# Decay sums and an evacuation moved to VectorE, the second weight loaded later, and a new fixed order, in a kernel of recurrent attention, Fourier mixing and an MLP

## Chip, cores and metric

One core of a Trainium2 chip. The metric is the device time of one execution in microseconds (us). Runs come with a state: a run over 1.5% above the fastest of the same kernel in its call is called slow and is left out of ratios. A **ratio** is the mean time of one kernel's fast runs over the mean of the other's fast runs of the same rounds, so it is not quite the ratio of the medians quoted beside it, which are of all runs, slow ones too. Intervals are of 95%.

Engines: PE is TensorE (matmuls; PEld its weight loads), DVE is VectorE, ACT is ScalarE, POOL is GpSimd, SP is SyncE, which issues loads and stores. PEclk is the share of full speed that the chip's throttle granted to TensorE.

## The reference

Four batches, eight heads, 768 steps, head size 48. A recurrence with a decay per step, then a 2D FFT over steps and features, a layer norm and an MLP (384 to 1536 to 384).

```python
for t in range(S):
    cur = einsum('bhd,bhe->bhde', u * k[t], v[t])
    y[t] = einsum('bhd,bhde->bhe', r[t], state + cur)
    state = w[t][..., None] * state + einsum('bhd,bhe->bhde', k[t], v[t])
x = y with the heads side by side                    # 4 x 768 x 384
u = x + real(fft(fft(x, axis=1), axis=2))
un = (u - mean) / sqrt(var + 1e-6)
out = u + relu(un @ w_ch1) @ w_ch2
```

## The kernel before

The recurrence is done in 24 chunks of 128 steps (6 to a batch; chunk 7 is the second of batch 1). Every operation of the program, 1540 of them, is recorded with its engine and dependencies; a constant list ORDER then says in which sequence they stand, and a constant BANKS which of the 8 PSUM banks each of 347 tiles gets. Each engine runs its own operations strictly in that sequence, and waits at each for what it depends on. So a wait on one engine holds up all that stands behind it.

The parts that the change touches, with cuts (`...`):

```python
def load(b, c):                                   # the SP queue
    for n in "wkrv":
        o = op("sp", "load", f, r=["W1"] if b*NC + c == NC + 1 and n == "w" else (), ...)

ws, WN = [], ((6, "w"), (6, "w"))                 # both weights are asked for when w of chunk 6 landed
def weights():                                    # GpSimd's queue
    ws.append(op("pool", "loadw", ... W1 ...)); ws.append(op("pool", "loadw", ... W2 ...))

KHD, DIAG, RKD, PRE, EVD = range(6), range(5), (), range(0), range(0)
TCD, SAD = range(12, 24), range(12, 24)

def attention(b, c):                              # n: the chunk's number
    tcd = n in TCD
    op("act", "ln", L = Ln(w))
    tce = g.tile(pool); tci = tce if tcd else g.tile(pool)
    op("pe", "cum", matmul(tce, MSK, L))          # L614: sums of decays up to a step
    if not tcd:
        op("pe", "cum", matmul(tci, NLE, L))      # L619: the other sum, by a second matmul
        op("act", "exp", exp of tce in place)
    ...
    if tcd:                                       # the other sum from the first, on DVE
        op("dve", "tcd", e2 = tce + L)            # L636
        op("act", "exp4", ...); op("act", "exp", ...); op("act", "expn", e2 = exp(-e2))
    elif early: ...
    else:
        op("act", "exp2", e2 = exp(tci))          # L648
    ...
    op("dve", "rh", rh = tce * r)                 # L663
    ...

def mix(b, ...):                                  # FFT, layer norm, MLP
    for kb in range(NC): ...
        op("dve", "uf", uf = mixed + x)
        op("pe", "trn", transpose of un) ...      # or, for the blocks of TUN, by a DMA on SP (L882)
        elif n in EVD: op("dve", "evd", unt <- PSUM)
        else:          op("act", "ev384", unt <- PSUM)
    for hf in range(2):
        for j in range(NJ):
            op("pe", "m1", 3 matmuls of W1 and unt)      # L920; L926 in the changed kernel
            ... relu to ht
        for x in range(3):
            for jq in range(3):
                op("pe", "m2", 4 matmuls of ht and W2)   # L941; L947 in the changed kernel
            op("dve", "osb", ...); op("sp", "store", ...)

NW2 = 5                                           # warm-up matmuls ahead of the first real work
...
g.arrange(ORDER, BANKS)
```

## Time and profile before

| | before |
|---|---|
| time, median of 3 runs | 196.43 us (195.55 to 197.74) |
| span of the profiled run | 193.5 us |
| busy: PE, DVE, ACT, POOL | 93%, 79%, 71%, 61% |
| mean granted clock | 1.00 |

In the page's span line and engine lines, x is the number of instructions. In a row of the windows, a stretch of time is followed by its length and the busy us of each engine in it. The lines on which the prediction rests are shown in it. One more is needed later, the shares of the chain of work that ended last:

```profile
PE 43%; DVE 34%; SPq 8%; DMA 6%; ACT 5%; issue 2%; DVEq 0%
```

### The profile page before, as it was taken

How to read it: one execution, taken by the hardware profiler on the slowest of the kernel's cores; microseconds unless marked ns; L12 is line 12 of the kernel's file. 1: busy time of each engine (PE TensorE's matmuls, PEld its weight loads, DVE VectorE, ACT ScalarE, POOL GpSimd, SP SyncE). 2: the span in 40 equal slices, each digit the busy share in tenths (PEclk: the TensorE clock that was granted, in tenths of full speed). 3: DMA queues.
4: the chain of work that ended last, by engine and by line, in shares of the span. 5: the costliest groups of instructions: out<-in, count | busy, mean ns of one | idle time of the engine just before them, and what ended most of it. 6: DMA issues, size and time to landing. Idle time of an engine off the chain costs nothing.

```text
span 193.5 us, 4590 instructions
## 1 busy us (share of the span) xinstructions
PE 180.0 (93%) x1730; PEld 114.7 (59%) x1730; DVE 152.1 (79%) x356; ACT 137.8 (71%) x333; POOL 118.3 (61%) x148
## 2 busy tenths in 40 slices
PE   4979899999999999998999998999979999979994
PEld 2446466755666566565767675666656566545663
DVE  8799689697258999999999999999989969800043
ACT  7899867656997794499999897488855344769400
POOL 1679789920689996899799988639375461000000
PEclk9999999999999999999999999999999999999999
DMA  5999899699989989889899991242735020140024
GB/s 118 225 217 188 170 218 172 116 179 201 208 176 237 207 176 244 160 193 233 186 211 227 199 226 32 54 125 54 160 68 122 3 81 2 38 149 0 0 81 163
DMA packets 113351, 28.14 MB, mean 145 GB/s; under 512 B 108209, under 2 KB 112946, under 8 KB 113330
## 3 DMA queue, kind: packets, MB, share of 16 engines
q1 hardware_dynamic: 111378, 25.50, 62.3%
q0 software_dynamic: 1952, 2.36, 7.4%
q8 instruction: 13, 0.21, 0.4%
q14 instruction: 8, 0.07, 0.1%
HBM read 23.59 MB, written 4.72 MB: 146 GB/s over the span
## 4 chain that ended last, share of the span: by engine, by line
PE 43%; DVE 34%; SPq 8%; DMA 6%; ACT 5%; issue 2%; DVEq 0%
PE bank L920 15%; PE bank L941 12%; SPq L440 7%; DVE ah L708 6%; DVE xf L404 5%; DVE x L862 4%; DVE osb L946 4%; DVE bst L866 3%; DMA unt<-un 3%; DMA in_w<-in_w_dram 3%; PE bank L821 3%; DVE x L773 2%; ACT ht L929 2%; DVE rh L663 2%; DVE xa L404 2%
## 5 line engine op out<-in xcount | busy, mean ns | idle before, releaser
L920 PE MATMUL bank<-unt,w 128*128 128x384 bf16 x288 | 52.5, 326 | 2.4 <-DMA unt<-un 2.4
L941 PE MATMUL bank<-w,ht 128*128 128x384 bf16 (+1 forms) x300 | 54.0, 320 | 0.2 <-DVE ah L708 0.2
L929 ACT ACTIVATE ht<-bank 128x384 bf16<-128x384 f32 x92 | 40.9, 505 | 9.8 <-PE bank L920 9.7
L920 PEld LDWEIGHTS bank<-unt,w 128*128 128x128 bf16 x288 | 26.4, 97 | 18.8 <-issue 3.2
L941 PEld LDWEIGHTS bank<-w,ht 128*128 128x128 bf16 x300 | 27.5, 98 | 15.3 <-DVE ah L708 0.4
L404 POOL TENSOR_TENSOR rk<-in_r,in_k 128x384 f32<-128x384 f32 x24 | 24.1, 1004 | 16.8 <-DMA in_r<-in_r_dram 15.8
L708 DVE TENSOR_TENSOR ah<-bank,msk 128x512 bf16<-128x512 f32 x48 | 31.2, 682 | 2.3 <-PE bank L703 2.2
L946 DVE SCALAR_TENSOR_TENSOR osb<-bank,rstd,x 128x384 f32<-128x384 f32 (+1 forms) x25 | 14.6, 595 | 21.7 <-PE bank L941 21.6
L404 POOL TENSOR_TENSOR rk<-rk,ub 128x384 f32<-128x384 f32 x24 | 24.2, 1013 | 0.6
L404 POOL TENSOR_TENSOR kh<-in_k,e 128x384 bf16<-128x384 f32 x18 | 18.3, 1019 | 5.8 <-ACT e L640 3.6
L404 POOL TENSOR_TENSOR vtd<-in_v,dc 128x384 f32<-128x384 f32 x24 | 19.8, 829 | 2.8 <-DVE dc L655 2.7
L663 DVE TENSOR_TENSOR rh<-bank,in_r 128x384 bf16<-128x384 f32 x24 | 13.2, 552 | 5.3 <-ACT bank L621 5.0
L418 ACT ACTIVATE un<-x,agg 128x384 bf16<-128x384 f32 x18 | 10.8, 619 | 9.3 <-DVE agg L868 9.1
L988 PE MATMUL bank<-wz 128*128 128x384 bf16 x53 | 13.8, 379 | 2.5 <-DVE wz L415 2.5
L655 DVE TENSOR_REDUCE dc<-rk 128x8 f32<-128x384 f32 x24 | 13.0, 545 | 1.9 <-POOL rk L404 1.8
L418 ACT ACTIVATE vb<-in_v 128x384 bf16<-128x384 f32 x24 | 12.7, 531 | 1.7 <-DMA in_v<-in_v_dram 1.2
L418 ACT ACTIVATE lb<-in_w 128x384 bf16<-128x384 f32 x24 | 12.6, 534 | 1.6 <-DMA in_w<-in_w_dram 1.3
L866 DVE BATCH_NORM_STATS2 bst<-x 128x6 f32<-128x384 f32 x24 | 12.7, 553 | 0.1
L821 PE MATMUL bank<-cs,xf 128*128 128x193 bf16 (+2 forms) x54 | 11.1, 257 | 1.4 <-DVE xf L404 1.2
L693 ACT ACTIVATE rtb<-bank 128x512 bf16<-128x512 bf16 x19 | 11.3, 605 | 1.4 <-PE bank L680 1.2
L862 DVE TENSOR_TENSOR x<-bank,x 128x384 f32<-128x384 f32 x24 | 12.3, 542 | 0.0
L695 ACT ACTIVATE ktb<-bank 128x512 bf16<-128x512 bf16 x19 | 11.2, 602 | 0.7 <-PE bank L684 0.7
(129 smaller groups left out, 362.3 us busy)
## 6 DMA issues: line engine op xcount, KB each, us to landing
in_w<-in_w_dram SPq DMA_DIRECT2D x24, 192.0 KB, 3.8
in_k<-in_k_dram SPq DMA_DIRECT2D x24, 192.0 KB, 3.8
in_r<-in_r_dram SPq DMA_DIRECT2D x24, 192.0 KB, 3.8
in_v<-in_v_dram SPq DMA_DIRECT2D x24, 192.0 KB, 3.9
out_dram<-osb SPq DMA_DIRECT2D x23, 192.0 KB, 2.3
w<-in_moe_w_ch_dram POOLq DMA_DIRECT2D x2, 1152.0 KB, 10.4
out_dram<-osb SPq DMA_DIRECT2D x2, 96.0 KB, 1.7
unt<-un SPq DMA_TRANSPOSE x6, 3.0
```

Of the source, the lines that this page charges most:

```text
L404: return shared(lambda e: e.tensor_tensor(out=o, in0=a, in1=b, op=f))
L418: return lambda e: e.activation(o, a, f, **kw)
L663: op("dve", "rh", lambda e: e.tensor_tensor(out=rh[:, :, 0:D], in0=ps(tce)[:, 0:DM].rearrange("t (h d) -> t h d", d=D), in1=rt[:, :, :], o ...
L708: masked[n] = op("dve", "ah", lambda e, x=x: e.tensor_tensor(out=ah[:, x:H:2, :], in0=ps(ta[x])[:, :].rearrange("p (h t) -> p h t", t=128) ...
L821: return e.matmul(ps(t)[:, k0:k1], xf[:, f, off:off + 128], tab[:, s, k0:k1], start=a, stop=z, skip_group_check=True)
L862: op("dve", "uf", lambda e, kb=kb, t=t: e.tensor_tensor(out=uf[:, kb, 0:DM], in0=ps(t)[:, 0:DM], in1=uf[:, kb, 0:DM], op=ALU.add), r=[t], ...
L866: op("dve", "bns", lambda e, kb=kb, bs=bs: e.bn_stats(bs[:, :], uf[:, kb, 0:DM]), r=[("X", b % 3, kb)], w=[("BST", n % 4)])
L920: ins = e.matmul(ps(t)[:, 0:384], W1[:, m, 128 * j:128 * j + 128], unt[:, m, :], start=(m == 0), stop=(m == NM - 1))
L929: op("act", "ev384", lambda e, j=j, t=t, ht=ht: e.activation(ht[:, j, :], ps(t)[:, 0:384], ACTF.Relu), r=[t], w=[("HT", q % 2, j)])
L941: ins = e.matmul(ps(t)[:, c0:c1], ht[:, j, 128 * x:128 * x + 128], W2[:, j, c0:c1], start=(j == 0), stop=(j == NJ - 1))
L946: op("dve", "osbh" if n_end else "osb", lambda e, kb=kb, t=t, o=o, c0=c0, c1=c1: e.scalar_tensor_tensor(out=o[:, c0:c1], in0=ps(t)[:, c0:c ...
L988: ins = e.matmul(ps(tw)[:, 0:384], WZ[:, 0:128], WZ[:, :])
```

## The change

The intent: from 44 to 60 us VectorE and GpSimd are half idle, because the load of the second weight holds up the inputs of chunk 7; later VectorE is full and TensorE waits for it. So ask for that weight later, and fill the hole with VectorE work that relieves TensorE, ScalarE and PSUM. The diff, cut to its core:

```diff
-            o = op("sp", "load", f, r=["W1"] if b * NC + c == NC + 1 and n == "w" else (), ...
+            o = op("sp", "load", f, r=[WG[b * NC + c]] if b * NC + c in WG and n == "w" else (), ...
-    ws, WN = [], ((6, "w"), (6, "w"))
+    ws, WN, WG = [], ((6, "w"), (9, "w")), {7: "W1"}
-    KHD, DIAG, RKD, PRE, EVD = range(6), range(5), (), range(0), range(0)
+    KHD, DIAG, RKD, PRE, EVD, PRM = range(6), range(5), (), (), range(3), ()
-    TCD, SAD = range(12, 24), range(12, 24)
+    TCD, SAD = range(6, 24), range(12, 24)
-    NW2 = 5
+    NW2 = 6
 ORDER, BANKS: new from the first entry to the last (1546 operations, 341 PSUM tiles)
```

PRM and PRE are empty, so what else the diff adds for them does nothing.

## The prediction

> **What bounds the kernel now.** I read the page first, then the work by stretch, the chain of work that ended last, the waits of 36 to 60 us, and the issues of the load queue.
>
> ```profile
> span 193.5 us, 4590 instructions
> PE 180.0 (93%) x1730; PEld 114.7 (59%) x1730; DVE 152.1 (79%) x356; ACT 137.8 (71%) x333; POOL 118.3 (61%) x148
> DMA  5999899699989989889899991242735020140024
> ```
> No engine is idle enough to make one bound for the whole kernel, and the DMA engines are full for the first 24 slices (116 us). PE's 93% is too high: its matmuls overlap. The chain shows
>
> ```profile
> 89.43 5.47 PE bank L920 x33
> ```
> which is 166 ns for a 384-column matmul whose row on the page says 326. So I count PE by 166 ns and look for where it waits.
>
> ```profile
> core 0: us, PE busy (x) PEld busy (x) DVE busy (x) ACT busy (x) POOL busy (x), PEclk, DMA share, GB/s
> 40.00:44.00 4.00, 3.72 (x34) 2.09 (x33) 3.93 (x12) 2.91 (x6) 0.00 (x0) 1.00 1.27 184
> 44.00:48.00 4.00, 4.00 (x28) 2.45 (x28) 3.05 (x10) 2.56 (x6) 0.00 (x0) 1.00 1.27 204
> 48.00:52.00 4.00, 4.00 (x34) 2.57 (x33) 1.11 (x2) 4.00 (x12) 1.99 (x2) 1.00 1.03 205
> 52.00:56.00 4.00, 4.00 (x34) 2.46 (x33) 1.02 (x2) 4.00 (x13) 3.70 (x5) 1.00 1.05 208
> 56.00:60.00 4.00, 4.00 (x43) 2.61 (x42) 3.13 (x6) 3.33 (x10) 3.23 (x5) 1.00 0.90 178
> 70.00:80.00 10.00, 9.57 (x113) 6.52 (x110) 9.86 (x21) 5.06 (x14) 7.86 (x10) 1.00 0.93 201
> 80.00:90.00 10.00, 8.99 (x99) 5.70 (x98) 9.88 (x24) 9.09 (x20) 9.67 (x13) 1.00 0.95 206
> ```
> Here is the hole. From 44 to 60 us DVE does 8.31 us of work in 16: 7.7 us idle, and GpSimd does nothing from 40 to 48. From 60 on DVE is full (19.36, 19.84, 19.35 and 19.66 us in the four 20 us stretches from 60 to 140) and PE has short stalls. The chain agrees: it runs through DVE from 60.3 to 88, through PE's MLP matmuls (L920, L941) from 89 to 113, again through DVE from 113 to 131. So work that DVE puts off at 44 to 60 is paid for later. Why the hole is there, the waits of that window tell:
>
> ```profile
> POOL rk L404 <- DMA in_r<-in_r_dram: 9.2, 1, 9.2
> DVE rh L663 <- ACT bank L621: 3.9, 2, 2.8
> DVE dc L655 <- POOL rk L404: 1.8, 1, 1.8
> ```
> and the load queue, where the column after the start is the length of an issue:
>
> ```profile
> 37.84 1.76 SPq L440 DMA_DIRECT2D in_r<-in_r_dram  x1
> 39.65 3.55 SPq L440 DMA_DIRECT2D in_v<-in_v_dram  x1
> 43.24 4.14 SPq L440 DMA_DIRECT2D in_w<-in_w_dram  x1
> 47.42 1.18 SPq L440 DMA_DIRECT2D in_k<-in_k_dram  x1
> ```
> The second weight is issued at 36.5 and lands 11.6 us later, at 48.1. The loads of chunk 7 go out in the same time and are held up: issues take up to 4.14 us instead of the median of 0.71, and r of chunk 7, issued at 37.8, is used only at 48.9.
>
> **What the Trainium skill says.** "DMA: Bandwidth & Descriptors", section "Issuing engines are not separate DMA queues": DMAs started by sync or gpsimd run on the same 16 engines and interleave. The trace agrees: the GpSimd queue's weight stretches the sync queue's loads as shown. "Perfetto Trace Analysis", section "Identifying the Most-Contended Engine": matmul busy share is a poor measure, matmuls being pipelined; the trace agrees (326 against 166 ns). "VectorE: DVE Perf Modes", section "The TRN2 errata", gives 120 + FD cycles for a one-per-cycle operation out of PSUM; at 384 elements and 0.96 GHz that is 525 ns. The decay sum L636 shows 551 ns, but two in a row take 0.97 us in the chain, so 0.48 each of the engine's time. I use 0.47.
>
> **The change, part by part.**
>
> Decay sums of batch 1 (chunks 6 to 11) on DVE. Removed from PE: 6 matmuls L619, 6 x 0.166 = 1.0 us. On ACT, 6 exponentials L648 (5 x 0.534 + 0.491 = 3.2 us) give way to 6 of L642 (0.529) and 5 short ones L640 (0.18): 3.2 + 0.9 = 4.1 us, so +0.9. Added on DVE: 6 x 0.47 = 2.8 us. One PSUM bank less is held per chunk. Latency to kh grows by about 0.5 us per chunk; it is hidden if the order runs ahead.
>
> Evacuation of the first half of batch 0: 3 copies of 128x384 leave ACT (L901, 0.42 us apart) and come to DVE, 3 x 0.47 = 1.4 us. They stand just before the first L920 (43.9 us), where DVE is full (3.93 of 4.00). In the new order they come after the statistics, so I expect the first L920 about 0.5 us later, at 44.4.
>
> Second weight after load 9: it is asked for when w of chunk 9 has landed. Chunks 7 and 8 (4 loads of 0.71 to 1 us of issue each) and w of 9 then take 36.8 to about 47, and r of chunk 7 lands at its normal 3.8 us, at about 42 instead of 48.9. The weight lands at 47 + 11.6 = 59 or so. In the new order all 24 first-layer matmul groups of batch 0 come ahead of the first L941 (before: at 52.7), so at 59 nobody waits for it yet. The bytes are the same; only their order changes.
>
> One more warm-up matmul: 0.17 us, where PE has slack. The parts named PRE and PRM have empty lists and do nothing. The W1 wait of the loads is the same one, spelled otherwise.
>
> Sum by engine: PE -0.8, DVE +4.2, ACT about -0.3.
>
> Fixed order anew. I counted what stands between the first L920 and the first finished L941 block (osb) in the new order. PE: 24 groups of 3 L920 (72 x 0.166 = 12.0), chunks 7 to 9 and half of 10 (1.65 us each: about 5.7), 12 L941 (2.0): 19.7 us. DVE: 46 instructions: 5 decay sums, 19 more of 384 elements (4 rh, 4 dc, 4 x, 4 relu, 2 uf, 1 fold) and 2 statistics at 0.47, 6 masks (L708) at 0.60, 8 half state products (L739) at 0.36, 6 small ones, together about 20 us. ACT: about 19.6 us. So the hole is to be filled, and all three engines are planned full at once. Before, DVE had done 8.9 us of work by the same output, at 60.3.
>
> Putting times on it: if nothing stalls, that output comes at 44.4 + 19.7 = 64. At that place DVE has finished chunk 9; in the kernel before it got there at 73.7, having done 3.0 us of other work by then, so at 70.7 like for like. DVE would be 6.7 ahead, including the extra sums. PE would be ahead by little: the hole was DVE's and GpSimd's; PE was 4.00 of 4.00 there. But three engines planned full with in-order queues don't run at 100%; I put 2 to 3 us of stalls there, an estimate by choice from PE's stalls in the stretches 80 to 90 (1.0 us of 10). That leaves DVE 4 us ahead and PE about 1 behind. What PE then wins is its stalls behind DVE between 60 and 88 and between 113 and 131: 0.4 and 1.0 us in the two rows shown, more when counted by 166 ns; I put 4 to 5 us. Some 3 of them go: -1 + 3 = 2, plus 0.3 from the removed matmuls and something from the second DVE-bound stretch. I expect 2.5 us less, at the end of which the tail (last transposes by DMA, then 72 matmuls of L920 and L941) is as before.
>
> **The rivals.**
> First, DVE becomes the bound by more: 4.2 us more work on an engine full from 60 to 140. If the hole isn't filled (ACT, 4.00 of 4.00 from 48 to 56, feeds rh; L663 waited 3.9 us for it there), the end moves by up to +3 us: 199. Against it: the new order puts chunk 7's exponentials ahead of the first-layer evacuations on ACT.
> Second, the full gain: stalls are few and PE keeps DVE's lead, 5 us or more less: 191. For it: the chain is DVE for 46 of the 71 us from 60 to 131. Against: PE's MLP stretch, 89 to 113, can't shrink.
> Third, the late weight is waited for: L941 stalls on W2 if load 9 lands after 50. Each us late past 62 is a us of PE: +1 to +3. Against: the first-layer matmuls and three chunks stand ahead of it.
> Fourth, the gain is swallowed by the tail: the DMA transposes (3.95 us in the chain before 173) and the fixed PE order: 196, no change.
>
> **Range and chances.** Before 196.43. The expected 2.5 us less (with the scatter of 1% of three runs) gives 193.8. The third and fourth rivals make 196 to 197, the second 191; so 190.8 to 196.8. Faster by over 2% needs 192.5: 0.27. Slower by over 2% needs the first rival in full: 0.05. Within 2%: 0.68.
>
> **What would show it.** Right: r of chunk 7 used at 42 to 43; GpSimd busy from there; DVE at least 13 of 16 us in 44 to 60; W2 landed by 60 with no wait of L941 for it; 6 L619 left; DVE full until about 128 instead of 131; chain in 60 to 88 partly PE. Wrong: DVE still idle by 5 us in 44 to 60 (stalls behind ACT), L941 waiting for the weight, or DVE's lead at 70 lost by 130.

## The result, and the profile after

| | before | after |
|---|---|---|
| time, median of 4 runs each | 197.09 us (195.55 to 199.55) | 189.83 us (188.88 to 191.57) |
| ratio of fast runs | | 0.9667 [0.9556, 0.9778] |

The result is correct and faster by 3.3%, outside the predicted range. In a later call the same kernel gave 0.9735 [0.9654, 0.9816], with 2 of 6 runs fast.

From the page of the changed kernel:

```profile
span 187.7 us, 4599 instructions
PE 179.4 (96%) x1725; PEld 115.5 (62%) x1725; DVE 155.4 (83%) x365; ACT 136.8 (73%) x335; POOL 118.6 (63%) x148
PEclk9969999999999999999999999999999999999999
PE 71%; SPq 8%; DVE 7%; DMA 7%; ACT 4%; issue 1%; DVEq 0%
```

DVE has 3.3 us more to do (155.4 against 152.1; 4.2 were forecast), PE 0.6 less, and the span is 5.8 us shorter. The chain went from one third DVE to nearly all PE. And there is a 6 in the clock's row, where before all slices had a 9: the third slice, 9.4 to 14.1 us. Both points get an experiment.

Work by stretch in the changed kernel, for the stretches shown of the kernel before:

```profile
core 0: us, PE busy (x) PEld busy (x) DVE busy (x) ACT busy (x) POOL busy (x), PEclk, DMA share, GB/s
40.00:44.00 4.00, 3.78 (x39) 2.36 (x38) 4.00 (x13) 2.98 (x7) 1.00 (x1) 1.00 1.11 222
44.00:48.00 4.00, 4.00 (x27) 2.25 (x25) 3.85 (x12) 3.85 (x12) 3.04 (x4) 1.00 1.05 202
48.00:52.00 4.00, 3.96 (x46) 2.67 (x46) 3.92 (x10) 4.00 (x12) 1.89 (x2) 1.00 1.11 206
52.00:56.00 4.00, 4.00 (x38) 2.37 (x38) 2.88 (x7) 4.00 (x12) 3.69 (x4) 1.00 1.24 172
56.00:60.00 4.00, 4.00 (x61) 2.74 (x57) 3.90 (x8) 4.00 (x11) 2.62 (x3) 1.00 1.26 193
70.00:80.00 10.00, 9.99 (x99) 6.59 (x97) 9.54 (x21) 5.71 (x15) 8.90 (x11) 1.00 0.83 187
80.00:90.00 10.00, 9.37 (x96) 5.79 (x94) 9.89 (x24) 9.18 (x22) 9.10 (x12) 1.00 1.08 215
```

The hole is filled: DVE does 14.55 us of work between 44 and 60 where it did 8.31, and GpSimd works from 42.3 on. From 70 to 90 TensorE is short of its length by 0.64 us (0.01 + 0.63) where it was by 1.44. The waits of 36 to 60 us have one entry left for the late r:

```profile
POOL rk L404 <- DMA in_r<-in_r_dram: 3.6, 1, 3.6
```

3.6 us instead of 9.2. The load queue says why (start, length of the issue):

```profile
38.76 0.58 SPq L440 DMA_DIRECT2D in_r<-in_r_dram  x1
...
52.32 5.16 SPq L440 DMA_DIRECT2D in_w<-in_w_dram  x1
57.52 4.42 SPq L440 DMA_DIRECT2D in_k<-in_k_dram  x1
```

The long issues have not gone; they have moved to 52 to 62 us, to chunks that nobody waits for yet. The second weight is issued at 48.8 and lands at 62.1, and the first weight load of L947, at 62.5, does not wait for it; the margin is 0.4 us.

So the first half went as predicted. But look at how far the changed kernel leads. The table gives the starts of three same instructions in the profiled run of each kernel: the first VectorE sum (uf) of block 0 of a batch's layer norm. The last two columns are spliced kernels of the experiments; the lead is against the kernel before.

| start, us (lead) | before | changed | old order to 84, new after | new order to 82, old after |
|---|---|---|---|---|
| batch 0 | 39.21 | 38.19 (1.02) | 38.22 (0.99) | 38.68 (0.53) |
| batch 1 | 83.98 | 81.79 (2.19) | 83.41 (0.57) | 82.28 (1.70) |
| batch 2 | 124.72 | 120.83 (3.89) | 121.90 (2.82) | 124.19 (0.53) |
| batch 3 | 162.59 | 156.91 (5.68) | 157.98 (4.61) | 161.60 (0.99) |

The third column has the same program as the kernel before up to 84 us, so its lead of 0.99 at batch 0 is scatter; differences down a column say more. For batches 1 and 3, block 0 stands at the same place of the batch in all four orders. For batches 0 and 2 it stands first in one order and second in another, which is worth 0.5 us, so those two rows are rougher. Between batch 1 and batch 3 the changed kernel wins 3.5 us (5.68 - 2.19), more than half of everything, in a part where the prediction expected next to nothing. Where, the stretches show in which PE is short of its length. Before:

```profile
110.00:120.00 10.00, 9.73 (x112) 6.73 (x109) 9.55 (x21) 8.74 (x22) 8.57 (x12) 1.00 0.70 155
120.00:130.00 10.00, 9.31 (x98) 6.14 (x99) 9.97 (x22) 5.65 (x14) 5.22 (x8) 1.00 0.36 87
...
140.00:150.00 10.00, 8.83 (x95) 5.73 (x94) 8.76 (x18) 5.53 (x14) 6.46 (x8) 1.00 0.45 97
150.00:160.00 10.00, 9.29 (x83) 5.85 (x81) 7.89 (x14) 4.22 (x10) 5.47 (x8) 1.00 0.12 41
...
170.00:180.00 10.00, 8.77 (x55) 5.11 (x54) 0.00 (x0) 8.18 (x25) 0.00 (x0) 1.00 0.22 70
```

After:

```profile
110.00:120.00 10.00, 10.00 (x108) 7.07 (x107) 9.57 (x22) 7.82 (x19) 7.86 (x11) 1.00 0.95 192
120.00:130.00 10.00, 10.00 (x86) 6.27 (x85) 9.96 (x24) 7.31 (x20) 8.57 (x11) 1.00 0.61 147
...
140.00:150.00 10.00, 10.00 (x109) 6.37 (x107) 9.66 (x22) 5.39 (x12) 6.28 (x9) 1.00 0.25 50
150.00:160.00 10.00, 10.00 (x79) 6.74 (x77) 6.96 (x16) 5.63 (x12) 3.52 (x6) 1.00 0.21 74
160.00:170.00 10.00, 9.02 (x56) 5.26 (x55) 4.05 (x13) 6.53 (x17) 0.00 (x0) 1.00 0.30 76
170.00:180.00 10.00, 10.00 (x64) 6.00 (x62) 1.24 (x2) 5.79 (x15) 0.00 (x0) 1.00 0.06 20
```

TensorE's idle time from 110 to 130 was 0.27 + 0.69 = 0.96 us and is 0; from 140 to 180 it was 1.17 + 0.71 + 1.23 = 3.11 us (none from 160 to 170) and is 0.98. What is gone are the 1.88 us of 140 to 160: the 1.23 us before and the 0.98 us after are the same wait for the last transpose, 5 us earlier. From the first uf of block 0 of batch 3 to the end, both kernels take the same time (193.5 - 162.59 = 30.9 and 187.7 - 156.91 = 30.8 us). A row of 10.00 can still hide short gaps, as matmuls overlap. What it waited for late in the kernel before is in the chain (start, us, what):

```profile
139.43 2.38 SPq L882
141.85 2.38 DMA unt<-un
...
144.37 0.65 PE bank L920 x3
...
156.63 1.31 DVE xf L404 x2
...
168.91 3.95 DMA unt<-un
...
173.10 1.95 PE bank L920 x11
```

Twice it is a normalised block (un) that has to go through a transpose by DMA before L920 can use it, and around 156 the folds (xf) on DVE. In the chain of the changed kernel TensorE runs through the first two places:

```profile
140.90 2.46 PE bank L926 x15
...
152.38 1.24 PE bank L821 x15
...
164.45 3.74 DMA unt<-un
...
168.43 5.52 PE bank L926 x33
```

Only the last transpose is left as a wait.

### The profile page after: what moved, and what is told of

Read it like the earlier page. It is cut to its first block, busy times and chain, and to the rows that moved or that the text cites. A ratio compares the mean times of both kernels' runs of the same rounds, so it can differ in the third digit from the quotient of the medians.

```text
span 187.7 us, 4599 instructions
## 1 busy us (share of the span) xinstructions
PE 179.4 (96%) x1725; PEld 115.5 (62%) x1725; DVE 155.4 (83%) x365; ACT 136.8 (73%) x335; POOL 118.6 (63%) x148
## 3 DMA queue, kind: packets, MB, share of 16 engines
q1 hardware_dynamic: 111378, 25.50, 64.1%
q0 software_dynamic: 1952, 2.36, 7.9%
## 4 chain that ended last, share of the span: by engine, by line
PE 71%; SPq 8%; DVE 7%; DMA 7%; ACT 4%; issue 1%; DVEq 0%
PE bank L947 23%; PE bank L926 20%; SPq L440 8%; PE bank L821 5%; PE bank L703 4%; PE bank L853 3%; DMA in_w<-in_w_dram 3%; PE bank L753 2%; PE bank L749 2%; DMA unt<-un 2%; DMA in_v<-in_v_dram 2%; PE bank L684 2%; DVE bst L869 2%; DVE x L862 2%; PE bank L614 2%; PE bank L680 2%
## 5 line engine op out<-in xcount | busy, mean ns | idle before, releaser
L947 PE MATMUL bank<-w,ht 128*128 128x384 bf16 (+1 forms) x300 | 54.0, 320 | 0.0
L947 PEld LDWEIGHTS bank<-w,ht 128*128 128x128 bf16 x300 | 27.5, 98 | 14.4
L994 PE MATMUL bank<-wz 128*128 128x384 bf16 x54 | 14.7, 387 | 1.2 <-DVE wz L415 1.2
L404 POOL TENSOR_TENSOR xd<-x 128x385 f32<-128x385 f32 x9 | 9.6, 1063 | 2.8 <-DVE x L773 2.7
## 6 DMA issues: line engine op xcount, KB each, us to landing
in_w<-in_w_dram SPq DMA_DIRECT2D x24, 192.0 KB, 3.8
in_k<-in_k_dram SPq DMA_DIRECT2D x24, 192.0 KB, 3.9
in_r<-in_r_dram SPq DMA_DIRECT2D x24, 192.0 KB, 3.9
in_v<-in_v_dram SPq DMA_DIRECT2D x24, 192.0 KB, 3.8
out_dram<-osb SPq DMA_DIRECT2D x23, 192.0 KB, 2.1
w<-in_moe_w_ch_dram POOLq DMA_DIRECT2D x2, 1152.0 KB, 11.1
```

The source lines that it names most:

```text
L404: return shared(lambda e: e.tensor_tensor(out=o, in0=a, in1=b, op=f))
L947: ins = e.matmul(ps(t)[:, c0:c1], ht[:, j, 128 * x:128 * x + 128], W2[:, j, c0:c1], start=(j == 0), stop=(j == NJ - 1))
L994: ins = e.matmul(ps(tw)[:, 0:384], WZ[:, 0:128], WZ[:, :])
```

## The experiments

**Theory A**, that of the prediction: the gain comes from the hole, by the late weight and the work moved into it. **Theory B**: it comes from the new order of the part after 84 us, which has nothing to do with the hole. **Theory C**: the bound has moved from DVE to PE, as the shares of the chain suggest, and that is the gain. Every kernel gave the correct result. The kernel before had a median of 195.2 to 195.9 us in these calls.

### The weight's time

`a_w2early`: the changed kernel with the old time of the weight, its request moved up accordingly in the order.

```diff
-    ws, WN, WG = [], ((6, "w"), (9, "w")), {7: "W1"}
+    ws, WN, WG = [], ((6, "w"), (6, "w")), {7: "W1"}
```

> The changed kernel with one thing undone: the second weight is asked for early again (after load 6, at its old place in GpSimd's queue, about 36 us); everything else, order included, as in the changed kernel. Theory 1 (the gain comes from the hole of 44 to 60 us, which the early weight makes): the loads of chunk 7 are held up again to about 48, DVE is idle 5 us or more in 44 to 60, and the time is 194 to 197 us, so most of the 6 us is lost. Theory 2 (half of the gain comes from the new order of batches 2 and 3): the hole's share alone is lost, 2 to 3 us: about 192.

Measured: 192.53 us, ratio 0.9855 [0.9769, 0.994]. The hole is back, and deeper:

```profile
44.00:48.00 4.00, 0.26 (x1) 0.13 (x2) 0.06 (x1) 0.93 (x2) 0.00 (x0) 0.94 1.20 207
```

TensorE and VectorE both stand still for nearly 4 us, GpSimd waits 9.5 us for r of chunk 7, and yet only 1.2 to 1.9% are lost against the changed kernel (0.9855 against 0.9735 to 0.9667). The new order needs the late weight, but over two fifths of the gain (1.45% of 3.3%) survive a hole worse than the old one.

`b_w2late`: the kernel before with the late weight alone.

```diff
-    ws, WN = [], ((6, "w"), (6, "w"))
+    ws, WN, WG = [], ((6, "w"), (9, "w")), {7: "W1"}
 ORDER: the weight's request behind the first products of chunk 8 and the load of w of chunk 9,
        and two groups of L947 matmuls, which need the weight, behind the request
```

> The kernel before with one thing done: the second weight after load 9, its place in GpSimd's queue moved behind chunk 8's rk; order otherwise as before. Both theories: the loads of chunks 7 and 8 land early, but the first second-layer matmuls stand in PE's queue at 52 us, so PE waits for the weight from about 54 to 60: slower than before or the same, 197 to 202 us. If it were faster, the late weight alone would be worth it and the order not needed.

Measured: 208.51 us, ratio 1.0663 [1.0578, 1.0748] (three fast runs; the profiled run was slow). Of its waits between 50 and 80 us:

```profile
PE bank L947 <- DMA w<-in_moe_w_ch_dram: 9.4, 1, 9.4
```

The old order wants the weight at 52.7 us and stops for it. This is the third rival of the prediction, true for the old order and not for the new one: the late weight is no gain of its own but a condition that the new order meets.

### Which half of the order

`b_then_a`: the kernel before with all its settings and its order up to the first uf of batch 1 (84 us), from there the order of the changed kernel (one PSUM tile in another bank). `a_then_b`: the changed kernel with its settings and order up to that place, then the old order (9 PSUM tiles had to get other banks).

```diff
 ORDER = entries of one kernel up to the first uf of batch 1
       + the remaining operations in the sequence of the other kernel
```

> The settings of the kernel before (early weight, decay sums of batch 1 on PE, evacuations on ScalarE), its own order up to the first uf of batch 1 (84 us), and from there the order of the changed kernel. Theory 1: no gain beyond 1 us, since DVE comes to 84 us as late as before: 195.5 to 197. Theory 2: the lead that grew after 84 us in the traces (from 2.2 to 5.7 us) comes from the order there: 3 us less, about 193.5.

> The settings of the changed kernel and its order up to the first uf of batch 1 (82 us), and from there the order of the kernel before. Theory 1: the lead of the first half is carried on and grows by itself, since DVE is ahead: 190 to 192. Theory 2: only the lead at 82 us is kept: 194 to 195. Nine PSUM banks had to be chosen anew at the seam, which may cost some tenths.

Measured: `b_then_a` 190.34 us (190.09 to 190.44), ratio 0.975 [0.9698, 0.9803]; `a_then_b` 193.33 us, 0.9885 [0.981, 0.996]. The kernel that has none of the settings and leaves the hole as it was gains 2.5%; the kernel that has the filled hole and the old rest gains 1.2%. The table above says the same of one run each: between batch 1 and batch 3, `b_then_a` wins 4.0 us (4.61 - 0.57) and `a_then_b` loses 0.7. TensorE in `b_then_a`:

```profile
80.00:90.00 10.00, 9.08 (x97) 5.65 (x96) 9.87 (x24) 8.98 (x21) 9.92 (x13) 1.00 1.04 215
...
110.00:120.00 10.00, 10.00 (x118) 7.12 (x114) 9.63 (x22) 7.81 (x20) 7.87 (x11) 1.00 0.65 135
120.00:130.00 10.00, 10.00 (x92) 6.39 (x87) 9.80 (x22) 7.30 (x19) 8.30 (x11) 1.00 0.63 151
...
140.00:150.00 10.00, 10.00 (x108) 6.33 (x107) 9.73 (x21) 5.40 (x12) 5.67 (x8) 1.00 0.26 52
150.00:160.00 10.00, 10.00 (x80) 6.76 (x78) 6.93 (x18) 4.56 (x10) 4.34 (x7) 1.00 0.17 61
```

Until 90 it is the kernel before; after 110 it is full like the changed kernel. Theory B holds for the larger part, theory A for the smaller.

The kept traces of all runs say it more sharply. Take the time from the first uf of batch 1 to the uf of block 0 of batch 3, in the profiled run of each kernel. All nine kernels that have the new order there and no work added take 74.5 to 75.2 us, whatever their settings, the time of the weight and the clock at the start. The kernels with the old order there take 78.5 to 79.3 us, also with the new order ahead (`a_then_b`, 79.3) or with the moves to VectorE (`b_tcd_evd`, 78.5); only the slow run of `b_w2late` lies outside, at 81.0. So the new order of this part is worth about 4 us by itself. The settings and the time of the weight show in the part ahead of it: the first uf of batch 1 comes at 83.98 us in the kernel before, at 81.79 in the changed kernel, but at 87.41 in `a_w2early`. Two cautions: `a_then_b` has the lower clock at the start that is shown further down and `b_then_a` has not, so the runs understate the smaller share somewhat; and "order" includes the PSUM banks that belong to it, which were not tested apart.

`b_then_a_124`: the splice at batch 2 (124 us; 18 PSUM tiles in other banks). `b_window`: new order only from 124 to 143 us.

> As the spliced kernel before, but with the old order kept up to the first uf of batch 2 (124 us) and the new one from there: 18 PSUM banks chosen anew at the seam. If the late gain comes from the shorter stalls of PE after 124 us (1.31 us at 144 for a transposed tile, 0.5, 0.3 and 0.4 at 153 to 158, 1.40 at 173), 2.5 to 3.5 us faster than the kernel before: ratio 0.982 to 0.987. If it comes from the folds of batch 2 (stalls of 0.47 and 0.81 at 120) and what stands before, under 1.5 us: 0.993 or more.

> The kernel before with the new order only between the first uf of batch 2 (124 us) and the first osb of batch 2 (143 us), old order ahead and behind. If the late sums of chunk 21 on DVE, behind which ScalarE keeps first-layer evacuations and the un tiles waiting, are what makes the 1.31 us stall at 144, that stall goes and 1 to 2 us are won: ratio 0.99 to 0.995. If not, 0.998 or more.

Measured: 191.99 us, 0.9867 [0.9813, 0.9921]; and 195.36 us, 1.0011 [0.9983, 1.0039]. About half of the late gain comes from each side of 124 us (2.5% with the splice at 84, 1.3% with the splice at 124), and the new order of 124 to 143 us alone gives nothing. I did not locate it more closely.

### The work moved to VectorE

`a_noevd`: the evacuation back on ScalarE. `a_notcd`: the decay sums of chunks 6 to 11 back on TensorE (42 tiles in other banks, as more are needed). `a_order_w2`: both back, so order and late weight alone. `b_tcd_evd`: both moves in the old order (12 tiles in other banks).

```diff
 a_noevd     -EVD = range(3)        +EVD = range(0)
 a_notcd     -TCD = range(6, 24)    +TCD = range(12, 24)
 a_order_w2  both of these
 b_tcd_evd   the kernel before with EVD = range(3), TCD = range(6, 24)
```

> The changed kernel with the three evacuations of batch 0's first half put back on ScalarE, order kept. If PE is the bound now and ScalarE is what feeds it at 44 to 60 (3.85 to 4.00 of 4.00 busy there), 1.3 us more on ScalarE delay the first-layer matmuls: 0.5 to 1 us slower than the changed kernel, about 190.5. If DVE is still the bound, 1.4 us less on DVE make it up to 1 us faster, about 188.8.

> The changed kernel with the decay sums of batch 1 back on PE (6 more matmuls, 6 exponentials of 388 columns, no DVE sums), the matmul placed right behind the other one in the order, 42 of 347 PSUM tiles in another bank than before, since six more tiles need one. PE-bound: +1.0 us for the matmuls and some tenths for the banks: 190.5 to 191.5. DVE-bound: 2.8 us less on DVE, 1 to 2 us faster, about 188.

> Both of these undone: new order and late weight alone. If the two moves to DVE matter little and the order (with the weight it allows for) is nearly all, 190 to 191.5, that is a ratio to the kernel before of 0.97 to 0.98. If the moves are what lets the order work, 193 or more.

> The kernel before with both moves to DVE alone (sums of batch 1, three evacuations), early weight, old order with the new instructions at the old ones' places. DVE was idle 7.7 us at 44 to 60 but the sums of chunks 9 to 11 fall behind 60, where it is full: if DVE bounds that kernel, 1 to 3 us slower, 196.5 to 198.5 at a before of 195.5. If PE bounds it, -1 us.

| kernel | median us | ratio |
|---|---|---|
| a_noevd | 191.57 | 0.9767 [0.971, 0.9824] |
| a_notcd | 192.9 | 0.9842 [0.9799, 0.9885] |
| a_order_w2 | 194.24 | 0.9902 [0.9868, 0.9937] |
| b_tcd_evd | 201.01 | 1.0243 [1.018, 1.0305] |

The same two moves are worth about -2% in the new order (0.9902 against 0.9667 to 0.9735) and cost 2.4% in the old. Their sum on the engines is the same in both cases. The intervals of `a_noevd` and of the changed kernel overlap, so the evacuation by itself is not shown to matter; for the decay sums, the changed kernel's runs at a clock of 0.991 took 188.5 to 189.6 us and those of `a_notcd` at 0.989 to 0.991 took 192.0 to 193.3. One caution: in `a_notcd`, `a_order_w2` and `b_tcd_evd` a part of the loss may be the other banks, and the order was made for other settings. In the traces the loss lies ahead of the first uf of batch 1 (85.00 us in `a_notcd`, 91.07 in `b_tcd_evd`). What follows is that settings and order are one choice, not that a decay sum is worth so much.

### Has the bound moved to TensorE?

`b_dve8`, `a_dve8`: one more DVE product beside rh in chunks 14 to 21, to a scratch tile (8 times 0.47 = 3.8 us). `b_pe24`, `a_pe24`: the cum matmul of the same chunks done four times (24 times 0.166 = 4.0 us).

```diff
 dve8  +  if 14 <= n < 22: e.tensor_tensor(out=SCR[:, n % 4], in0=tce, in1=rt, op=mult)
 pe24  +  for _ in range(4 if 14 <= n < 22 else 1): matmul(tce, MSK, L)
```

> The kernel before with 8 more DVE instructions, one beside each rh of chunks 14 to 21 (95 to 135 us), same operands, to a scratch tile nobody reads: 8 x 0.47 = 3.8 us of DVE. If DVE bounds that kernel there, as its chain says, most of it shows: 2.5 to 4 us slower, 198 to 200 at a before of 195.5.

> The same 8 instructions in the changed kernel (190 us, ratio to the kernel before 0.967). If the bound has gone from DVE to PE, as its chain says (PE 71%, DVE 7%), DVE has slack and less than 1.5 us of the 3.8 shows: ratio up to 0.975. If DVE still bounds it, 3 us or more: ratio 0.982 and over.

> The kernel before with each cum matmul of chunks 14 to 21 done four times: 24 more matmuls of 0.166 us, 4.0 us of PE. If DVE bounds that kernel, part of it is hidden in PE's stalls: 1 to 2.5 us slower. If PE bounds it, 3.5 to 4 us.

> The same 24 matmuls in the changed kernel. If PE bounds it, 3.5 to 4 us slower, ratio 0.985 to 0.988. If not, 2 us or less, ratio up to 0.977.

| added | to the kernel before | to the changed kernel |
|---|---|---|
| 3.8 us on DVE | 197.08 us, 1.0102 [1.0033, 1.0171] | 191.09 us, 0.9783 [0.9718, 0.9847] |
| 4.0 us on PE | 198.64 us, 1.0176 [1.0119, 1.0232] | 194.0 us, 0.9929 [0.9898, 0.9961] |

In the kernel before, DVE's work costs 2.0 us of its 3.8 and PE's 3.5 of its 4.0 (fast means, 197.14 and 198.62 against 195.16). In the changed kernel, against 0.9667 to 0.9735 without an addition, DVE's costs 0.5 to 1.2% and PE's 1.9 to 2.6%. The intervals are wide, but the traces agree: from the first uf of batch 1 to that of block 0 of batch 3, where all the added work stands, DVE's costs 2.8 us before and 1.7 after, PE's 4.1 and 3.4. Both kernels feel both engines. The changed one may feel DVE somewhat less, but by nothing like the fall of the chain's share of DVE from 34% to 7%. The kernel before felt PE's work nearly in full already, so theory C is not supported: the shares of a chain tell where the last wait was, not what a us is worth.

### Can the changed kernel's own stall at 85 us be taken away?

`a_plus`: two operations moved to shorten TensorE's stall: a copy on ScalarE (vb of chunk 14) behind un of block 1 of batch 1, and a store on SP behind the loads of chunk 14.

```diff
 ORDER (changed kernel): vb of chunk 14 behind un of block 1 of batch 1; store of block 2 of batch 0 behind the loads of chunk 14
```

> The changed kernel with two instructions moved: the cast of v of chunk 14 on ScalarE (it waits for its load to 82.3 us and holds up un of batch 1, for which PE waits 0.70 and 0.58 us at 84.8 to 86.7) behind un, and the store of the third output tile behind the loads of chunk 14. If PE's stalls are the time, 0.7 to 1.3 us faster than the changed kernel, 188.5 to 189; if they are made up later, no difference.

`ctrl_after`: the changed kernel again, in the same call.

> The changed kernel itself once more, for comparison on the same chip in the same rounds: ratio to the kernel before 0.965 to 0.972.

Measured: 190.5 us, 0.976 [0.9714, 0.9806], against 0.9735 [0.9654, 0.9816] for the control. No gain, but the edit missed its aim as well. Of `a_plus`:

```profile
80.00:90.00 10.00, 8.26 (x88) 5.01 (x86) 9.38 (x22) 8.19 (x20) 8.94 (x11) 1.00 1.08 214
```

TensorE now idles 1.74 us there instead of 0.63. So the run says nothing of what taking the stall away would bring. Nor does it show that more idle time there is free: its span of 187.9 us is near the changed kernel's 187.7 of the first call, but 1.3 us above the 186.6 of `ctrl_after`, the control of its own call, all three at a clock of 0.991.

### The start, and the scatter

Every kernel with the new start showed clocks of 0.97 to 0.99 and times that scatter with them (`a_order_w2`: 192.6 to 193.4 us in six of seven fast runs at 0.989 to 0.991, 194.6 to 195.4 at 0.971 to 0.974); those with the old start had 1.00 in nearly all runs. The exception is `b_w2late`, with 0.967 to 0.975 in every run: while TensorE waited 9.4 us for the weight, its clock fell to 0.50. In the new order the memset of the warm-up tile is the fourth operation of VectorE, before it was the fourteenth. From the timeline of TensorE in the changed kernel:

```profile
1.24 5.04 PE L994 MATMUL bank<-wz 128*128 128x384 bf16 x16 [1.24 <-DVE wz L415]
7.61 0.88 PE L481 MATMUL bank<-ht 1*128 1x384 f32 x2 [1.33 <-DVE ht L415]
```

The warm-ups end at 6.28, and TensorE idles 1.33 us before its first real matmul. In the kernel before they start at 2.51 and run into it. The changed kernel's clock (third number from the end):

```profile
6.00:8.00 2.00, 0.67 (x3) 0.29 (x2) 1.61 (x7) 1.89 (x4) 1.72 (x3) 1.00 1.11 223
8.00:10.00 2.00, 2.00 (x20) 1.27 (x18) 2.00 (x7) 1.98 (x6) 0.71 (x1) 0.82 1.12 215
10.00:12.00 2.00, 1.63 (x18) 1.20 (x15) 2.00 (x5) 1.97 (x7) 2.00 (x3) 0.50 1.07 213
```

`a_head`: the changed kernel with that one memset back in fourteenth place. `b_warmearly`: the kernel before with it in fourth place.

```diff
 ORDER: one entry moved, the memset of wz
```

> The changed kernel with one VectorE instruction moved: the memset of the warm-up tile goes back from place 4 to place 14 of VectorE's order, as the kernel before has it. The 16 warm-up matmuls should then start at about 2.4 us instead of 1.24 and run into the first real matmul at about 7.6 us without the gap of 1.33 us. Theory 'the gap lets the clock drop': granted clock 1.00 in every slice from 8 to 16 us, no run with a mean clock under 0.985, about 188 to 189 us, ratio 0.960 to 0.968, scatter under 1 us. Rival 'the drop at 8 to 16 us has another cause, or costs nothing': clocks of 0.97 to 0.99 as in the changed kernel, 189 to 192 us, ratio 0.967 to 0.976.

> The kernel before with that memset moved forward to place 4 of VectorE's order: the warm-ups start at about 1.2 us, end at about 6.3, and TensorE idles about 1.2 us until its first real matmul at 7.4. Theory 'the gap lets the clock drop': granted clock of 0.5 to 0.9 somewhere in 8 to 16 us, mean 0.97 to 0.99, time up by 1 to 2 us, ratio 1.005 to 1.010. Rival 'another cause': clock 1.00 throughout, ratio 0.998 to 1.002.

Measured: `a_head` 188.88 us, 0.97 [0.9664, 0.9736]; four of six runs at clock 1.00 and 188.35 to 188.94 us, the other two, slow, at 0.98 and 191.5 and 192.2. `b_warmearly` 195.23 us, 1.0007 [0.9981, 1.0032]; the clock was below 0.998 in 18 of 22 runs, where the kernel before beside it had that in 1 of 27. In `a_head`, the warm-ups run from 3.09 to 7.51, and the clock holds:

```profile
6.00:8.00 2.00, 1.87 (x9) 0.93 (x8) 1.61 (x7) 1.89 (x4) 1.76 (x3) 1.00 1.18 230
8.00:10.00 2.00, 1.93 (x20) 1.05 (x18) 2.00 (x7) 1.98 (x5) 0.68 (x1) 1.00 1.15 224
10.00:12.00 2.00, 1.17 (x15) 0.85 (x16) 2.00 (x5) 2.00 (x8) 2.00 (x3) 1.00 1.11 210
```

And in `b_warmearly` it drops, though the expected gap is not there: its first real matmul follows the warm-ups at once, and the only waits of TensorE from there to 9 us are 0.75 and 0.48 us.

```profile
6.00:8.00 2.00, 1.18 (x4) 0.20 (x3) 2.00 (x7) 1.40 (x3) 1.77 (x4) 1.00 1.11 223
8.00:10.00 2.00, 1.53 (x16) 1.07 (x17) 0.88 (x3) 1.89 (x5) 0.41 (x1) 0.61 1.08 213
10.00:12.00 2.00, 2.00 (x18) 1.92 (x17) 1.99 (x6) 2.00 (x8) 2.00 (x3) 0.53 1.10 213
```

So the place of that memset decides in most runs whether the clock drops, both ways; what exactly about the early warm-ups does it is not shown. My theory was half right: it also said that the drop costs 1 to 2 us in the kernel before, and no cost is seen there. In the changed kernel the short drop of the profiled run costs little: in the two profiled runs, the first uf of batch 0 comes at 37.40 us in `a_head` and at 38.19 in the changed kernel, and of batch 3 at 156.03 and 156.91, so 0.8 to 0.9 us; the four fast runs of `a_head` (188.35 to 188.94) and the runs of the changed kernel at 0.991 (188.53, 188.88, 189.58) are hardly apart.

But the drop is not always short. The clock's row of `a_dve8`, whose profiled run was slow (193.6 us, the fast ones 190.7 to 191.1), is also that of `a_noevd` and `a_order_w2`:

```profile
PEclk9756999999999999999999999999999999999999
```

The stretches of 2 us put the clock at 0.50 for about 3.4 us in the changed kernel, 6.8 in `a_then_b` and 10.2 in these three, and these are the runs of mean clock 0.991, 0.982 and 0.971 to 0.973. TensorE's idle time behind the warm-ups grows in the same sequence: 1.33, 1.95 and 2.36 to 2.48 us. With 10.2 us the first uf of block 0 of batch 0 comes at 40.6 to 41.2 us, about 3 us later than the 37.40 of `a_head`. The ten runs of the changed kernel follow their clock: 188.5 to 189.6 us at 0.991, 190.1 at 0.982, 191.2 to 192.2 at 0.971 to 0.973. So much of the scatter among the kernels with the new start, their slow runs included, goes with the length of the drop at the start; that it is caused by it is likely, but no run tests it. It also means that ratios of these kernels depend on how many of their runs had the long drop. The slow runs of the kernel before at a clock of 1.00 (196.8 to 197.7 us) are something else, and their cause stays open.

`a_head`, with its clock at 1.00 in its fast runs, is the steadiest measure of what the change is worth, -3.0%, and is faster than both kernels by its median; that it beats the changed kernel is not shown by the intervals.

## Why the prediction was wrong

**Right, step by step.** r of chunk 7 was to be used at 42 to 43: it was at 42.34. DVE at least 13 of 16 us in 44 to 60: 14.55. No wait of L941 for the weight: nobody waited, though it landed at 62.1 and not by 60, 13.3 us after its issue where 11.6 was assumed. Six L619 left. The first finished output block was to come at 64.1 plus 2 to 3 us of stalls: it came at 67.22. VectorE was to be 6.7 us ahead without stalls and 4 with them: it began its last product of chunk 8 at 65.19 instead of 71.78, 6.6 us earlier, and that of chunk 9 5.9 us earlier. By the prediction's own measure, that output block, it is 70.7 - 67.2 = 3.5 us. The tail was to stay as it was, and it did (30.9 and 30.8 us from the uf of block 0 of batch 3 on). One sign failed: VectorE was to be full until about 128 us instead of 131, but was busy 9.66 of 10 us as late as 140 to 150. Two small slips in the text: 196.43 - 2.5 is 193.9, not 193.8, and the 525 ns worked out from the skill's cycles is an estimate (measured: 551 ns).

**Right in size for that part.** 2.5 us less was expected, but for the whole kernel, the stalls of 113 to 131 included, so that the sizes agree so well is in part luck. At the first uf of batch 1 the lead was 2.19 us, and the kernel with the new first part and the old rest gains 1.15% [0.4, 1.9], 2.2 us. One term was off: the first L920 did not come 0.5 us later but at 43.8, as before.

**The step that failed** is the one from there to the end: "Some 3 of them go: -1 + 3 = 2, plus 0.3 from the removed matmuls and something from the second DVE-bound stretch". It took the new order as a means to fill the hole, counted its instructions only between the first L920 and the first output block, and let the rest of the kernel stand. The stalls it listed were 60 to 88 and 113 to 131, and it read the chain only up to 131. But from 131 to 170 the chain of the kernel before has 19 us of DVE, 8 of ACT and 6 of transposes by DMA and their issue, and only 5 of PE. TensorE idled 1.88 us there, from 140 to 160; in the changed kernel this idle time and all 0.96 us of 110 to 130 are gone, and the stretch between batches 1 and 3 is 3.5 us shorter. `b_then_a` shows that the order after 84 us does this with the hole left as it was: 2.5%, against 1.15% for the first part. The two add up to 3.65%, a little above the 2.65 to 3.3% of the whole.

**The rivals.** The second rival, the full gain of 191, was nearest in size, but for another reason than it gave. The third was true of the old order (+6.6%). The first, that more DVE work makes the kernel slower, was true of the old order as well (+2.4%, `b_tcd_evd`), a clear sign that the order decides what a move of work is worth. That DVE as the bound is the reason there is not shown: in that kernel DVE was busy for only 7.63 of 10 us from 60 to 70, where it was 9.50 before.

**Open.** Which moves within the new order after 84 us bring the gain: the splice at 124 us splits it in halves, the window from 124 to 143 us has none of it by itself. What the new PSUM banks alone are worth. Why the drop of the clock at the start is longer in some runs, and what makes the slow runs at a clock of 1.00.

## What to carry to other kernels

When a change comes with a new fixed order, the order is a change of its own, everywhere: take TensorE's idle time of every stretch before, up to the last, and ask of each whether the new order can reach it. Splice the two orders at a place where both have done the same work; that separates the order from the settings in two runs. And don't read the value of a us on an engine from its share of the chain: add a few us and measure.

## What the Trainium skill lacked or had wrong

- "TensorE: Matmul & The Clock Gate", section "HAM oscillation — how this bites in real kernels", gives as its rule "no PE-idle gaps >~3.4µs". Here warm-ups that ended at 6.28 us and a gap of 1.33 us before the next matmul went with a granted clock of 0.50 at 10 to 12 us, and gaps of 2.36 to 2.48 us with one of 0.50 for about 10 us; in `b_warmearly` it fell with no gap over 0.75 us from the warm-ups to 9 us. Without that gap (`a_head`) the clock stayed at 1.00, though TensorE was busy for only 1.17 of 2.00 us at 10 to 12. So keeping to that rule was not enough here.
- "DMA: Bandwidth & Descriptors", section "Issuing engines are not separate DMA queues", calls the time to initiate a DMA "usually small relative to the DMA itself". While the weight moved on GpSimd's queue, issues on SyncE's queue took 4.42 and 5.16 us in the changed kernel, where the median is 0.8, longer than the 3.8 us from issue to landing of such a load otherwise. That an issue can be held up so long is on no page. (What made the hole is the load itself: in the kernel before, r of chunk 7 was issued at 37.84 and used at 48.94, 11.1 us later.)
- No page says how a chain of waits relates to sensitivity: DVE had 34% of the chain in one kernel and 7% in the other, and 3.8 us more on it cost 1.0% and 0.5 to 1.2%.
- No page tells of slow runs of one core at an undisturbed clock: 196.8 to 197.7 us at 1.00 beside 193.3 to 196.0, in the kernel before of the last call.
